# Five places for the raw weight tiles, paired down products and another order of the PSUM banks

## The chip, the cores and the metric

The kernel runs on one core of a Trainium2 chip. Its time is the device time of one execution in microseconds (us). TensorE (PE in the rows) does the matmuls, VectorE (DVE) and ScalarE (ACT) the work on their results, GpSimd (POOL) work from SBUF to SBUF, and SyncE (SP) issues nearly all transfers. Each engine takes its instructions in the written order.

## The reference, cut to what matters

```
x = attention(q, k, v)                     # 4 batches x 8 heads, 576 positions, block-causal
x = square(relu(x @ w_in1)) @ w_out1       # 2304 x 512 -> 2048 -> 512
h = x @ w_in2
g = (a0 + a1 h + a2 h^2 + a3 h^3) / (1 + |b0||h| + |b1| h^2 + 1e-6)
out = g @ w_out2                           # 2304 x 512 -> 2048 -> 512
```

## The kernel before

**Products in two parts.** Each float32 operand is split into a rounded high part and a rest, and a product is three matmuls (`PAIRS`, L129). PE therefore carries nearly all the work.

**Stages.** The first feed-forward layer is cut along its 2048 hidden columns into 16 blocks of 128 (index m). Stage A, `moe_a` (L472), does blocks 0 to 7 (HALF) for one batch at a time, in two sub-blocks of 320 and 256 tokens: eight up products `ha`, each followed by `relu_square` (L515), and then four down products `ya`, one for each 128 output columns c. Its work for batches 0 to 2 is laid between the instructions of the attention, step by step; the last batch stands alone, after the attention. The sums `ya` go to DRAM (`yp`). Stage B (from L722) does blocks 8 to 15 for all tokens in blocks of 384 and 512 (`hb`, `yb`) and adds `yp`. Stage C (from L780) is the second layer (`hc`, `yc`).

**Weights.** They arrive as 64-bit words. `Converter` (L81) turns a raw tile (512 KB, `raw`) into float32 (`cv`: one ACT and four DVE instructions, L119 to L125) and, a step later, into the two parts (`w`: L112 on ACT, L113 on POOL). One converter does each group of weights: `convA` those of stage A, `convB` (L664) twelve of the sixteen of stage B, `conv3` (L695) the rest and stage C's. A raw tile is loaded by SP (L93) into one of three places (four in `conv3`), and a place is free when the conversion of the tile in it has ended. A step that carries gates (`tc.issue_after`) is ordered behind the named instructions.

**Order.** `TileContext` orders the instructions by a simulated schedule and adds the semaphores, so the order on the engines follows from the code and the gates together. `convB` has its first three steps gated on the attention's slot 64 (`gate_b`) and the later ones on the last step of `moe_a` (`paced`).

**PSUM.** Eight banks. In stage A and the attention they are divided by name: three `tp`, one `sy`, two `mm`, two `sx`. Stages B and C take all eight anew: four `h` and four `y`.

The names in the rows leave the numbers out: `raw_bi`, `raw_bo` are raw tiles of `convB` or of the four stage-B tiles of `conv3` (i: up, o: down weights), `cv_bi` the float32 tile, `w_bi` the parts, `ga`, `gb` the squared values, `yo` the evacuated `ya`.

Of the kernel before, what the change touches and what calls it, by code (L numbers as in the profile page):

```python
# [8 lines left out]
F32 = mybir.dt.float32  # L9
F32R = mybir.dt.float32r  # L10
U32 = mybir.dt.uint32
AF = mybir.ActivationFunctionType
# [5 lines left out]
P = 128  # L18
S = 576
# [3 lines left out]
KK = DM // P  # L23
DFF = 2048
NM = DFF // P
HALF = NM // 2
HS = S // 2
NB = 12
# [3 lines left out]
SUB = 320  # L32
# [17 lines left out]
def attention_moe_moe(ctx: ExitStack, tc: tile.TileContext, q, k, v, wi1, wo1, wi2, wo2, a, b, out):  # L50
    nc = tc.nc
    NH_ALL = q.shape[0]
    H = DM // D
    B = NH_ALL // H
# [8 lines left out]
    yp = dram.tile([P, KK, NT], F32, name="yp")  # L63
# [12 lines left out]
        name=nc.get_next_instruction_name(), act_func_set_id=EXP_LN_SET, ins=[], outs=[]))  # L76
# [4 lines left out]
    class Converter:  # L81

        def __init__(self, pool, nraw, nmid, jobs):
            self.pool, self.nraw, self.nmid, self.jobs = pool, nraw, nmid, list(jobs)
            self.raws, self.mid = [], []

        def load(self, most=9):
            while self.jobs and len(self.raws) < min(self.nraw, most):  # L90
                job = self.jobs.pop(0)
                raw = self.pool.tile([P, 512, 2], U32, tag="wraw", name=f"raw_{job[0]}", bufs=self.nraw)
                nc.sync.dma_start(raw.rearrange("p n t -> p (n t)"), job[1])  # L93
                self.raws.append((raw, job))

# [3 lines left out]
        def __call__(self, *gates):  # L99
            with ExitStack() as after:  # L100
                for g in gates:
                    after.enter_context(tc.issue_after(g.ins))
                self.step()

        def step(self):
            if len(self.mid) == self.nmid or (self.mid and not self.raws):
                c, (nm, _, wp, kind, store, key, eng) = self.mid.pop(0)
                if wp is None:
                    nc.sync.dma_start(store[key], c)
                else:  # L110
                    w = wp.tile([P, 2, 512], F32R, tag="w" + kind, name=f"w_{nm}", bufs=HALF)
                    nc.scalar.activation(w[:, 0, :], c, AF.Copy)  # L112
                    eng.tensor_tensor(w[:, 1, :], c, f(w[:, 0, :]), op=ALU.subtract)  # L113
                    store[kind, key] = w
            if self.raws:
                raw, job = self.raws.pop(0)
                c = self.pool.tile([P, 512], F32, tag="cv", name=f"cv_{job[0]}", bufs=self.nmid + 1)
                low, high, cu = raw[:, :, 0], raw[:, :, 1], c.bitcast(U32)
                nc.scalar.activation(c, high.bitcast(F32), AF.Abs, scale=65536.0)  # L119
                nc.vector.tensor_scalar(low, low, 2.0 ** -29, 7.0, op0=ALU.mult, op1=ALU.min)  # L120
                nc.vector.scalar_tensor_tensor(
                    low, high, 0x80000000, low, op0=ALU.bitwise_and, op1=ALU.bitwise_or)
                nc.vector.tensor_scalar(c, c, 2.0, 122880.0 * 65536.0, op0=ALU.max, op1=ALU.min)
                nc.vector.scalar_tensor_tensor(
                    cu, cu, 3, low, op0=ALU.logical_shift_left, op1=ALU.bitwise_or)  # L125
                self.mid.append((c, job))
            self.load()

    PAIRS = ((0, 0), (1, 0), (0, 1))  # L129

# [333 lines left out]
    wA = {}  # L464
# [5 lines left out]
    paced = ()  # L470

    def moe_a(b_):  # L472
        nonlocal paced
        turn = 0

        def bank(nm):
            nonlocal turn
            turn += 1
            tag = "tp" if b_ == B - 1 and turn % 2 else "mm"
            return ps1.tile([P, 512], F32, tag=tag, name=nm, bufs=BANKS[tag])  # L480

        xt = xtile[b_]
        for s, (first, end) in enumerate(SUBS):
            n = end - first
            gs = []
            for m in range(HALF):
                ps = bank(f"ha{b_}_{s}_{m}")
                w = wA["i", m]
                for i in range(3 * KK):
                    kk, (zw, zx) = i // 3, PAIRS[i % 3]  # L490
                    nc.tensor.matmul(ps[:, 0:n], w[:, zw, P * kk:P * (kk + 1)], xt[:, zx, kk, first:end],  # L491
                                     start=i == 0, stop=i == 3 * KK - 1)
                    if i % 3 == 2 and i < 3 * KK - 1:
                        yield
                g = g1.tile([P, 2, SUB], F32R, tag="g", name=f"ga{b_}_{s}_{m}", bufs=HALF)
                paced = relu_square(lambda tag, nm: tmp1(n, nm), ps[:, 0:n], g[:, :, 0:n], f"{b_}_{s}_{m}", nc.gpsimd,
                            b_ == B - 1 and s == 1)[:2]
                gs.append(g)
                yield
            for c in range(KK):  # L500
                ps = bank(f"ya{b_}_{s}_{c}")
                for i in range(3 * HALF):
                    m, (zw, zg) = i // 3, PAIRS[i % 3]
                    nc.tensor.matmul(ps[:, 0:n], wA["o", m][:, zw, P * c:P * (c + 1)], gs[m][:, zg, 0:n],  # L504
                                     start=i == 0, stop=i == 3 * HALF - 1)
                    if i % 3 == 2 and i < 3 * HALF - 1:
                        yield
                y = g1.tile([P, n], F32, tag="ya", name=f"yo{b_}_{s}_{c}", bufs=2, padded_shape=[P, SUB])
                paced = (nc.scalar.activation(y, ps[:, 0:n], AF.Copy),)
                nc.sync.dma_start(yp[:, c, S * b_ + first:S * b_ + end], y)  # L510
                yield
        xtile.pop(b_)


# [9 lines left out]
    for gis, heads in (((0, 1), range(H)), ((2, 3), range(H)), ((0, 1, 2, 3), range(H, NH_ALL))):  # L524
# [3 lines left out]
    units_at = {un.at: n for n, un in enumerate(units)}  # L528
    NI = len(slots)
    PER_B = 4 * H  # L530
    convA = Converter(g1, 3, 1, [
        (f"a{kind}{m}", src[m], wpool, kind, wA, m, nc.gpsimd)
        for kind, src in (("i", wi1), ("o", wo1)) for m in range(HALF)])

    load_qk(units[0], nc.scalar)
    load_qk(units[1])
# [124 lines left out]
    jobsB = [(f"b{kind}{m}", src[HALF + m], w2, kind, wB, m, nc.gpsimd)  # L661
             for m in range(HALF) for kind, src in (("i", wi1), ("o", wo1))]

    convB = Converter(g1, 3, 1, jobsB[:NB])  # L664
    n = 0
    SPLITS = (73, 80, 87, 94)
    x_first = load_x(xs, *blocks2[0], "b0")
# [19 lines left out]
    def tmp(tag, n, nm, dt=F32):  # L687
# [4 lines left out]

    late = [(kind, m) for m in range(HALF, NM) for kind in "io"]
    source = {"i": wi2, "o": wo2}
    conv3 = Converter(g2, 4, 2, jobsB[NB:] + [  # L695
        (f"c{kind}{m}", source[kind][m], None, kind, waiting, n, nc.gpsimd) for n, (kind, m) in enumerate(late)] + [
        (f"c{kind}{m}", source[kind][m], wpool, kind, w3, m, nc.gpsimd) for m in range(HALF) for kind in "io"])

# [25 lines left out]
    END = 2  # L724
    SPLIT_AT = len(blocks2) * HALF - 4
    done = ()
    acc = {}
    units = [(j, m) for j in range(len(blocks2)) for m in range(HALF)]
    xt = {0: x_first}
    gs, ypart = {}, {}  # L730
# [1 line left out]
    for u in range(len(units) + LAG):  # L732
        if u < len(units):
            j, m = units[u]
            t0, n = blocks2[j]
            nxt = (xs, *blocks2[j + 1], f"b{j + 1}") if j + 1 < len(blocks2) else (xs2, *blocks3[0], "c0")
            if m == 0:
                xt[j + 1] = load_x(*nxt)
            ps = h_matmul(wB["i", m], xt[j], n, f"b{j}_{m}")
            g = g2.tile([P, 2, 512], F32R, tag="g", name=f"gb{j}_{m}", bufs=3)  # L740
            done = relu_square(lambda tag, nm: tmp(tag, n, nm), ps[:, 0:n], g[:, :, 0:n], f"b{j}_{m}", nc.vector, True)
            gs[u] = g
            if 2 <= m < 2 + KK:
                with tc.issue_after(done[1].ins):
                    split_x(xt[j + 1], m - 2, nxt[2])
        if u >= LAG:
            j, m = units[u - LAG]
            t0, n = blocks2[j]
            g = gs.pop(u - LAG)
            last = m == HALF - 1  # L750
            if m == HALF // 2:
                for c in range(KK):
                    ypart[c] = tmp("t" if c < 3 else "o", n, f"yp{j}_{c}")
                    nc.sync.dma_start(ypart[c], yp[:, c, t0:t0 + n])
            for c in range(KK):
                if m == 0:
                    acc[j, c] = psh.tile([P, 512], F32, tag="y", name=f"yb{j}_{c}", bufs=4)
                for i, (zw, zg) in enumerate(PAIRS):
                    nc.tensor.matmul(acc[j, c][:, 0:n], wB["o", m][:, zw, P * c:P * (c + 1)], g[:, zg, 0:n],  # L759
                                     start=m == 0 and i == 0, stop=last and i == 2)  # L760
            if last:
                for c in range(KK):
                    y = ypart[c]
                    done = nc.vector.tensor_tensor(y, acc.pop((j, c))[:, 0:n], y, op=ALU.add),
                    nc.sync.dma_start(xs2[:, c, t0:t0 + n], y)


        if u < 3 or u in (4, 6) or u > 6:
            conv3(*done)
        at = u - (len(units) - HALF) - 1  # L770
        for kind, m in (("i", at), ("o", at - LAG)):
            if 0 <= m < HALF:
                load_late(kind, HALF + m)
        split_late(u - SPLIT_AT, done)
# [139 lines left out]
```

## Time and profile before

| | us |
|---|---|
| median of 3 runs | 1015.86 (1014.85 to 1016.08) |
| the profiled execution, its own time | 1015.24 |
| its span, first to last instruction | 1013.5 |
| PE busy in the span | 997.2 (98%) |
| PE idle in the three waits of 375 to 435 us | 0.69, 0.68, 0.71 |

The attention with stage A laid into it runs to about 364 us of the span, the last batch of stage A from there to 412.7, stage B to about 610, stage C to the end. PE busy counts a matmul from its start to its modelled end, and the next one starts before that end, so an idle time in a row is a little shorter than what PE lost. The granted clock is 1.00 in all stretches.

### The profile page before, as it was taken

How to read it: one execution, taken by the hardware profiler on the slowest of the kernel's cores; microseconds unless marked ns; L12 is line 12 of the kernel's file. 1: busy time of each engine (PE TensorE's matmuls, PEld its weight loads, DVE VectorE, ACT ScalarE, POOL GpSimd, SP SyncE). 2: the span in 40 equal slices, each digit the busy share in tenths (PEclk: the TensorE clock that was granted, in tenths of full speed). 3: DMA queues.
4: the chain of work that ended last, by engine and by line, in shares of the span. 5: the costliest groups of instructions: out<-in, count | busy, mean ns of one | idle time of the engine just before them, and what ended most of it. 6: DMA issues, size and time to landing. Idle time of an engine off the chain costs nothing.

```text
span 1013.5 us, 17096 instructions
## 1 busy us (share of the span) xinstructions
PE 997.2 (98%) x5745; PEld 884.1 (87%) x5745; DVE 760.5 (75%) x1413; ACT 727.5 (72%) x1621; POOL 589.1 (58%) x632
## 2 busy tenths in 40 slices
PE   8999999999999999999999999999999999999998
PEld 6678998999999999999888888878888888899997
DVE  6899698768787656777768786888877667677766
ACT  7789686868877746655446566778787876778775
POOL 5777695868686755421114276865574564565552
PEclk9999999999999999999999999999999999999999
DMA  9866435243332204658754652001101100200000
GB/s 284 257 195 211 127 108 162 75 120 106 109 93 88 66 18 161 218 154 278 267 196 144 210 182 76 1 1 42 42 0 32 42 1 1 73 1 1 32 1 32
DMA packets 63895, 106.60 MB, mean 105 GB/s; under 512 B 16064, under 2 KB 34496, under 8 KB 63808
## 3 DMA queue, kind: packets, MB, share of 16 engines
q1 hardware_dynamic: 63520, 105.34, 33.3%
q8 instruction: 46, 0.75, 0.3%
q14 instruction: 41, 0.34, 0.1%
q10 hardware_dynamic: 288, 0.16, 0.1%
HBM read 79.17 MB, written 23.07 MB: 101 GB/s over the span
## 4 chain that ended last, share of the span: by engine, by line
PE 80%; DVE 7%; ACT 6%; DMA 3%; issue 2%; POOL 1%; SPq 0%; ACTq 0%; DVEq 0%; POOLq 0%
PE yc L839 17%; PE hc L718 16%; PE yb L759 9%; PE hb L718 9%; PE ha L491 7%; PE ya L504 7%; PE tp L379 4%; PE pv L451 4%; PE sx L303 3%; PE sy L303 2%; DMA raw_bo<-in_wo_dram 2%; PE pv L438 1%; DVE stat L324 1%; DVE ab L806 1%; DVE wq L805 1%
## 5 line engine op out<-in xcount | busy, mean ns | idle before, releaser
L718 PE MATMUL hc<-xc,w_ci 128*128 128x512 f32 (+1 forms) x960 | 210.9, 368 | 0.0
L718 PEld LDWEIGHTS hc<-xc,w_ci 128*128 128x128 f32 x960 | 176.4, 188 | 26.3
L839 PE MATMUL yc<-w_co,gc 128*128 128x512 f32 x792 | 194.3, 392 | 0.6 <-ACT gc L798 0.5
L839 PEld LDWEIGHTS yc<-w_co,gc 128*128 128x128 f32 x792 | 147.4, 188 | 32.4 <-POOL gc L799 2.1
L799 POOL TENSOR_TENSOR gc<-t,gc 128x512 fp32r<-128x512 f32 (+1 forms) x70 | 97.1, 1392 | 117.0 <-issue 68.6
L491 PE MATMUL ha<-xt,w_ai 128*128 128x320 f32 (+1 forms) x768 | 122.5, 305 | 0.5 <-POOL xt L460 0.5
L504 PE MATMUL ya<-ga,w_ao 128*128 128x320 f32 (+1 forms) x768 | 116.7, 299 | 1.4 <-POOL ga L521 0.7
L491 PEld LDWEIGHTS ha<-xt,w_ai 128*128 128x128 f32 x768 | 107.6, 189 | 5.1 <-issue 3.0
L504 PEld LDWEIGHTS ya<-ga,w_ao 128*128 128x128 f32 x768 | 106.4, 189 | 3.3 <-POOL ga L521 1.0
L822 POOL TENSOR_TENSOR wq<-wq,ab 128x512 f32<-128x512 f32 (+1 forms) x78 | 93.6, 1201 | 23.9 <-ACT wq L820 22.7
L759 PE MATMUL yb<-gb,w_bo 128*128 128x512 f32 (+1 forms) x480 | 105.8, 368 | 0.9 <-DVE gb L521 0.9
L718 PE MATMUL hb<-xb,w_bi 128*128 128x512 f32 (+1 forms) x480 | 105.2, 367 | 0.0
L759 PEld LDWEIGHTS yb<-gb,w_bo 128*128 128x128 f32 x480 | 87.5, 188 | 13.0 <-DVE gb L521 1.6
L718 PEld LDWEIGHTS hb<-xb,w_bi 128*128 128x128 f32 x480 | 87.4, 188 | 11.1
L823 DVE TENSOR_TENSOR t<-hc,t 128x512 f32<-128x512 f32 (+1 forms) x80 | 50.9, 637 | 59.6 <-ACT t L821 59.6
L805 DVE SCALAR_TENSOR_TENSOR wq<-wq,ab 128x512 f32<-128x512 f32 (+1 forms) x80 | 64.3, 804 | 36.9 <-ACT ab L804 22.2
L365 POOL TENSOR_SCALAR p<-p,stat 64x64 f32<-64x64 f32 (+4 forms) x110 | 64.5, 588 | 42.6 <-DVE stat L361 10.9
L798 ACT ACTIVATE gc<-t 128x512 fp32r<-128x512 f32 (+1 forms) x72 | 43.0, 597 | 62.4 <-DVE t L807 62.3
L411 DVE TENSOR_TENSOR pt<-tp,pt 128x128 fp32r<-128x128 f32 (+2 forms) x176 | 63.2, 391 | 27.1 <-ACT pt L409 16.8
L379 PE MATMUL tp<-ident,p 128*128 128x128 f32 x480 | 77.1, 276 | 0.3 <-ACT xp L446 0.3
L409 ACT ACTIVATE pt<-tp 128x128 fp32r<-128x128 f32 (+2 forms) x176 | 57.1, 362 | 26.6 <-PE tp L379 25.0
L657 POOL TENSOR_TENSOR xb<-xb 128x512 fp32r<-128x512 f32 (+1 forms) x20 | 25.4, 1268 | 75.6 <-ACT xb L656 75.6
(146 smaller groups left out, 2110.3 us busy)
## 6 DMA issues: line engine op xcount, KB each, us to landing
kr<-in_k_dram SPq DMA_DIRECT2D x32, 288.0 KB, 3.7
raw_ci<-in_wi_dram SPq DMA_DIRECT2D x16, 512.0 KB, 4.2
raw_co<-in_wo_dram SPq DMA_DIRECT2D x16, 512.0 KB, 4.1
qr<-in_q_dram SPq DMA_DIRECT2D x24, 320.0 KB, 3.4
raw_ai<-in_wi_dram SPq DMA_DIRECT2D x8, 512.0 KB, 5.8
raw_ao<-in_wo_dram SPq DMA_DIRECT2D x8, 512.0 KB, 4.1
raw_bi<-in_wi_dram SPq DMA_DIRECT2D x8, 512.0 KB, 3.7
raw_bo<-in_wo_dram SPq DMA_DIRECT2D x8, 512.0 KB, 4.2
```

The source lines that it names most:

```text
L365: nc.gpsimd.tensor_scalar(pv, pv, st[r:P, 6 + n:7 + n], 0.0, op0=ALU.mult, op1=ALU.add)
L379: nc.tensor.transpose(ps[:, P * n:P * (n + 1)], ptile(slots[i][0], t)[:, P * c:P * (c + 1)], ident)
L409: nc.scalar.activation(high, src, AF.Copy)
L411: nc.vector.tensor_tensor(low, src, f(high), op=ALU.subtract)
L491: nc.tensor.matmul(ps[:, 0:n], w[:, zw, P * kk:P * (kk + 1)], xt[:, zx, kk, first:end], start=i == 0, stop=i == 3 * KK - 1)
L504: nc.tensor.matmul(ps[:, 0:n], wA["o", m][:, zw, P * c:P * (c + 1)], gs[m][:, zg, 0:n], start=i == 0, stop=i == 3 * HALF - 1)
L718: nc.tensor.matmul(ps[:, 0:n], w[:, zw, P * kk:P * (kk + 1)], xt[:, zx, kk, 0:n], start=i == 0, stop=i == 3 * KK - 1)
L759: nc.tensor.matmul(acc[j, c][:, 0:n], wB["o", m][:, zw, P * c:P * (c + 1)], g[:, zg, 0:n], start=m == 0 and i == 0, stop=last and i == 2)
L799: (nc.vector if u - 2 >= len(units) - END else nc.gpsimd).tensor_tensor(g[:, 1, 0:n], t, f(g[:, 0, 0:n]), op=ALU.subtract)
L805: nc.vector.scalar_tensor_tensor(w, w, Q0, r, op0=ALU.add, op1=ALU.mult)
L822: squared = (nc.vector if u >= len(units) - END else nc.gpsimd).tensor_tensor(w, w, ab, op=ALU.mult)
L839: last = nc.tensor.matmul(acc[j, c], g[:, zg, P * c:P * (c + 1)], w3["o", m][:, zw, :], start=m == 0 and i == 0, stop=m == NM - 1 and i == 2)
```

## The change

`Converter` takes two sets of places: `bufs` and `more`, the second under a tag of its own. `convB` gets 3 + 2 places for raw tiles, 2 + 1 for `cv`, and `nmid` 2 instead of 1, so that the parts `w` are made two steps after `cv`. The first use of each added raw place has a memset of two words in front of its load. In `convB` (after its first load) and `conv3` a load is written outside the gates of its step. `convA` and `conv3` keep their number of places; `convA` loads inside the gates as before.

In the last batch of stage A the down products go in pairs: blocks 0 to 6 for c, blocks 0 to 6 for c + 1, and only then block 7 of both.

The `y` banks of stage B are taken before the `h` banks, which moves `h` from banks 0 to 3 to banks 4 to 7.

```
-    def __init__(self, pool, nraw, nmid, jobs):
-        self.pool, self.nraw, self.nmid, self.jobs = pool, nraw, nmid, list(jobs)
+    def __init__(self, pool, bufs, more, nmid, jobs, ahead=True):
+        self.raws, self.mid, self.turn, self.ahead = [], [], [0, 0], ahead
+        self.nraw = bufs[0] + more[0]
+    def place(self, which, shape, dt, tag, name):
+        own, more = self.bufs[which], self.more[which]
+        spare = self.turn[which] % (own + more) >= own
+        self.turn[which] += 1
+        return self.pool.tile(shape, dt, tag=tag + "2" if spare else tag, name=name, bufs=more if spare else own)
...
-                raw = self.pool.tile([P, 512, 2], U32, tag="wraw", name=f"raw_{job[0]}", bufs=self.nraw)
+                raw = self.place(0, [P, 512, 2], U32, "wraw", f"raw_{job[0]}")
+                if self.bufs[0] < self.turn[0] <= self.nraw:
+                    nc.vector.memset(raw[:, 0, :].bitcast(F32), 0.0)
                 nc.sync.dma_start(raw.rearrange("p n t -> p (n t)"), job[1])
...
                 self.step()
+                if not (self.ahead and self.turn[0]):
+                    self.load()
+            self.load()
...
-            self.load()
...
-            for c in range(KK):
-                ps = bank(f"ya{b_}_{s}_{c}")
...
+            step = 2 if b_ == B - 1 else 1
+            for c0 in range(0, KK, step):
+                cs = range(c0, c0 + step)
+                ps = {c: bank(f"ya{b_}_{s}_{c}") for c in cs}
+                order = [(c, m) for c in cs for m in range(HALF - 1)] + [(c, HALF - 1) for c in cs]
...
-    convB = Converter(g1, 3, 1, jobsB[:NB])
+    convB = Converter(g1, (3, 2), (2, 1), 2, jobsB[:NB])
...
-    acc = {}
+    acc = {(0, c): psh.tile([P, 512], F32, tag="y", name=f"yb0_{c}", bufs=4) for c in range(KK)}
```

**What it moves on PE, first sub-block of the last batch.** The names: `ya_0_0` and `ya_0_1` are the down products c = 0 and 1, `ga_0_7` is the last block's value. Before:

```order
L504 MATMUL ya_0_0_5651<-ga_0_6_5613,w_ao_1279 128x320
L504 MATMUL ya_0_1_5690<-ga_0_1_5494,w_ao_911 128x320
L504 MATMUL ya_0_1_5690<-ga_0_2_5514,w_ao_987 128x320 x3
L504 MATMUL ya_0_1_5690<-ga_0_3_5542,w_ao_1045 128x320 x2
L504 MATMUL ya_0_0_5651<-ga_0_7_5644,w_ao_1381 128x320 x2
L504 MATMUL ya_0_1_5690<-ga_0_3_5542,w_ao_1045 128x320
L504 MATMUL ya_0_1_5690<-ga_0_4_5562,w_ao_1115 128x320 x3
L504 MATMUL ya_0_1_5690<-ga_0_5_5593,w_ao_1200 128x320 x2
L504 MATMUL ya_0_0_5651<-ga_0_7_5644,w_ao_1381 128x320
L504 MATMUL ya_0_1_5690<-ga_0_5_5593,w_ao_1200 128x320
```

The same place now:

```order
L518 MATMUL ya_0_0_5654<-ga_0_6_5616,w_ao_1279 128x320
L518 MATMUL ya_0_1_5655<-ga_0_1_5500,w_ao_911 128x320 x3
L518 MATMUL ya_0_1_5655<-ga_0_2_5520,w_ao_987 128x320 x3
L518 MATMUL ya_0_1_5655<-ga_0_3_5548,w_ao_1045 128x320 x3
L518 MATMUL ya_0_1_5655<-ga_0_4_5568,w_ao_1115 128x320 x3
L518 MATMUL ya_0_1_5655<-ga_0_5_5596,w_ao_1200 128x320 x3
L518 MATMUL ya_0_1_5655<-ga_0_6_5616,w_ao_1279 128x320 x3
L518 MATMUL ya_0_0_5654<-ga_0_7_5647,w_ao_1381 128x320 x3
L518 MATMUL ya_0_1_5655<-ga_0_7_5647,w_ao_1381 128x320 x3
```

The third matmul on `ga_0_7`, the one that needs POOL's part of it, was the 41st of the down products and is now the 45th.

**What it moves on ACT, end of stage A.** The names: `yo_1_2`, `yo_1_3` are the copies of the last two down products, `w_b..` and `cv_b..` steps of `convB`, `rb_0` the first instruction of stage B. Before:

```order
L509 ACTIVATE yo_1_0_6040<-ya_1_0_6004 128x256
L509 ACTIVATE yo_1_1_6068<-ya_1_1_6043 128x256
L112 ACTIVATE w_bi_6071<-cv_bi_6031 128x512
L119 ACTIVATE cv_bo_6074<-raw_bo_5935 128x512
L509 ACTIVATE yo_1_2_6105<-ya_1_2_6080 128x256
L112 ACTIVATE w_bo_6112<-cv_bo_6074 128x512
L509 ACTIVATE yo_1_3_6136<-ya_1_3_6108 128x256
L517 ACTIVATE rb_0_6175<-hb_0_6161 128x384
```

Now:

```order
L522 ACTIVATE yo_1_0_6061<-ya_1_0_6003 128x256
L522 ACTIVATE yo_1_1_6067<-ya_1_1_6004 128x256
L124 ACTIVATE w_bo_6070<-cv_bo_5984 128x512
L131 ACTIVATE cv_bo_6073<-raw_bo_5818 128x512
L124 ACTIVATE w_bi_6108<-cv_bi_6031 128x512
L124 ACTIVATE w_bo_6138<-cv_bo_6073 128x512
L522 ACTIVATE yo_1_2_6129<-ya_1_2_6079 128x256
L522 ACTIVATE yo_1_3_6135<-ya_1_3_6080 128x256
L530 ACTIVATE rb_0_6181<-hb_0_6167 128x384
```

The last step of `convB` stood between the copies `yo_1_2` and `yo_1_3`; now both copies stand behind it, and four instructions of `convB` lie between `yo_1_1` and `yo_1_2`, where two did.

**What it moves on DVE, in the attention near slot 64.** The names: `stat`, `sy`, `tp`, `pt` belong to the attention, the rest to `convB`. Before:

```order
L360 TENSOR_SCALAR stat_131<-stat_131 128x2
L361 RECIPROCAL stat_131<-stat_131 128x2
L324 TENSOR_REDUCE stat_133<-sy_2443 128x1
L123 TENSOR_SCALAR cv_bi_5525<-cv_bi_5525 128x512
L123 TENSOR_SCALAR cv_bo_5579<-cv_bo_5579 128x512
L411 TENSOR_TENSOR pt<-tp_0_2373,pt 128x3x128
```

Now:

```order
L371 TENSOR_SCALAR stat_131<-stat_131 128x2
L132 TENSOR_SCALAR raw_bi_5484<-raw_bi_5484 128x512
L372 RECIPROCAL stat_131<-stat_131 128x2
L335 TENSOR_REDUCE stat_133<-sy_2443 128x1
L135 TENSOR_SCALAR cv_bi_5531<-cv_bi_5531 128x512
L133 SCALAR_TENSOR_TENSOR raw_bi_5484<-raw_bi_5484 128x512
L135 TENSOR_SCALAR cv_bo_5582<-cv_bo_5582 128x512
L422 TENSOR_TENSOR pt<-tp_0_2373,pt 128x3x128
```

Two instructions on the raw tile of the second added place (`raw_bi_5484`) come in front of the attention's `pt`; the two memsets stand 16 rows earlier. SP issues the loads of both added places here, behind a `kr` load.

## Rows read from the trace of the kernel before

**Rows 1.** The page, busy time of each engine in the span.
```profile
PE 997.2 (98%) x5745; PEld 884.1 (87%) x5745; DVE 760.5 (75%) x1413; ACT 727.5 (72%) x1621; POOL 589.1 (58%) x632
```
**Rows 2.** Waits of PE, whole span: total us, times, longest us.
```profile
PE sy L303 <- ACT p L337: 3.0, 3, 1.5
...
PE yb L759 <- DVE gb L521: 0.9, 2, 0.7
...
PE ya L504 <- POOL ga L521: 0.7, 1, 0.7
PE ya L504 <- ACT r L517: 0.7, 1, 0.7
PE ha L491 <- POOL xt L460: 0.5, 1, 0.5
```
**Rows 3.** Timeline of PE, 365 to 440: start us, length us, instructions, idle before.
```profile
373.10 6.03 PE L504 MATMUL ya<-ga,w_ao 128*128 128x320 f32 x40
379.82 8.48 PE L504 MATMUL ya<-ga,w_ao 128*128 128x320 f32 x56 [0.69 <-POOL ga L521]
388.14 11.68 PE L491 MATMUL ha<-xt,w_ai 128*128 128x256 f32 x96
...
402.29 10.39 PE L504 MATMUL ya<-ga,w_ao 128*128 128x256 f32 x81 [0.68 <-ACT r L517]
...
432.46 2.01 PE L759 MATMUL yb<-gb,w_bo 128*128 128x384 f32 x10 [0.71 <-DVE gb L521]
```
**Rows 4.** Matmul groups of PE by shape: busy us, mean ns of one.
```profile
L504 PE MATMUL ya<-ga,w_ao 128*128 128x320 f32 x384 | 64.3, 313 | 0.7 <-POOL ga L521 0.7
L504 PE MATMUL ya<-ga,w_ao 128*128 128x256 f32 x384 | 52.4, 286 | 0.7 <-ACT r L517 0.7
```
**Rows 5.** Timelines of DVE and POOL, 376 to 380.
```profile
376.53 1.52 DVE L123 TENSOR_SCALAR cv_bi<-cv_bi 128x512 f32<-128x512 f32 x1
...
376.01 1.75 POOL L113 TENSOR_TENSOR w_bo<-cv_bo,w_bo 128x512 fp32r<-128x512 f32 x1
378.59 1.18 POOL L521 TENSOR_TENSOR ga<-s,ga 128x320 fp32r<-128x320 f32 x1 [0.82 <-DVE s L520]
```
**Rows 6.** Timelines of ACT and DVE, 398 to 402.
```profile
401.34 0.63 ACT L112 ACTIVATE w_bo<-cv_bo 128x512 fp32r<-128x512 f32 x1 [2.41 <-DVE cv_bo L124]
401.87 0.37 ACT L517 ACTIVATE r<-ha 128x256 f32<-128x256 f32 x1
...
398.56 0.95 DVE L120 TENSOR_SCALAR raw_bo<-raw_bo 128x512 uint32<-128x512 uint32 x1 [0.91 <-DMA raw_bo<-in_wo_dram]
```
**Rows 7.** Timelines of ACT, SP and DVE, 415 to 431.
```profile
415.07 0.63 ACT L112 ACTIVATE w_bo<-cv_bo 128x512 fp32r<-128x512 f32 x1 [1.59 <-DVE cv_bo L124]
415.61 0.37 ACT L509 ACTIVATE yo<-ya 128x256 f32<-128x256 f32 x1
...
416.37 0.42 SPq L93 DMA_DIRECT2D raw_bi<-in_wi_dram  x1
...
430.77 2.11 DVE L521 TENSOR_TENSOR gb<-sb,gb 128x384 fp32r<-128x384 f32 x2
```
**Rows 8.** Timelines of SP, DVE and POOL in the attention, 161 to 174.
```profile
161.06 0.38 SPq L202 DMA_DIRECT2D kr<-in_k_dram  x1
...
167.40 0.62 DVE L324 TENSOR_REDUCE stat<-sy 128x1 f32<-128x448 f32 x1 [0.38 <-PE sy L303]
...
171.98 1.92 POOL L249 TENSOR_TENSOR kk<-kr,kk 64x576 fp32r<-64x576 f32 x1
```
**Rows 9.** Groups of DVE by shape: busy us, mean ns of one.
```profile
L121 DVE SCALAR_TENSOR_TENSOR raw_bi<-raw_bi 128x512 uint32<-128x512 uint32 x8 | 8.3, 1036 | 0.1
...
L120 DVE TENSOR_SCALAR raw_bi<-raw_bi 128x512 uint32<-128x512 uint32 x8 | 5.9, 742 | 7.0 <-DMA raw_bi<-in_wi_dram 6.9
...
L267 DVE MEMSET stat<- 128x8 f32 x8 | 0.2, 65 | 0.0
```
**Rows 10.** The line that issues the raw loads, issue to landing, 64 loads.
```profile
DMA to landing us min/median/max: 3.3/4.1/7.9
```

More of the change, by code (lines that the diff above doesn't have):

```diff
@@ L81, in attention_moe_moe @@
     class Converter:
-        def __init__(self, pool, nraw, nmid, jobs):
-            self.pool, self.nraw, self.nmid, self.jobs = pool, nraw, nmid, list(jobs)
-            self.raws, self.mid = [], []
+        def __init__(self, pool, bufs, more, nmid, jobs, ahead=True):
+            self.pool, self.bufs, self.more, self.nmid, self.jobs = pool, bufs, more, nmid, list(jobs)
+            self.raws, self.mid, self.turn, self.ahead = [], [], [0, 0], ahead
[5 more added lines that the diff above has]
+            return self.pool.tile(shape, dt, tag=tag + "2" if spare else tag, name=name, bufs=more if spare else own)
         def load(self, most=9):
@@ L116, in step @@
                 raw, job = self.raws.pop(0)
-                c = self.pool.tile([P, 512], F32, tag="cv", name=f"cv_{job[0]}", bufs=self.nmid + 1)
+                c = self.place(1, [P, 512], F32, "cv", f"cv_{job[0]}")
                 low, high, cu = raw[:, :, 0], raw[:, :, 1], c.bitcast(U32)
@@ L499, in moe_a @@
                 yield
-            for c in range(KK):
-                ps = bank(f"ya{b_}_{s}_{c}")
[L502 to L511, printed above, removed]
+            step = 2 if b_ == B - 1 else 1
[3 more added lines that the diff above has]
+                order = [(c, m) for c in cs for m in range(HALF - 1)] + [(c, HALF - 1) for c in cs]
+                for c, m in order:
+                    for i, (zw, zg) in enumerate(PAIRS):
+                        nc.tensor.matmul(ps[c][:, 0:n], wA["o", m][:, zw, P * c:P * (c + 1)], gs[m][:, zg, 0:n],
+                                         start=m == 0 and i == 0, stop=m == HALF - 1 and i == 2)
+                    if m == HALF - 1:
+                        y = g1.tile([P, n], F32, tag="ya", name=f"yo{b_}_{s}_{c}", bufs=2, padded_shape=[P, SUB])
+                        paced = (nc.scalar.activation(y, ps[c][:, 0:n], AF.Copy),)
+                        nc.sync.dma_start(yp[:, c, S * b_ + first:S * b_ + end], y)
+                    yield
         xtile.pop(b_)
@@ L530, in attention_moe_moe @@
     PER_B = 4 * H
-    convA = Converter(g1, 3, 1, [
+    convA = Converter(g1, (3, 2), (0, 0), 1, [
         (f"a{kind}{m}", src[m], wpool, kind, wA, m, nc.gpsimd)
-        for kind, src in (("i", wi1), ("o", wo1)) for m in range(HALF)])
+        for kind, src in (("i", wi1), ("o", wo1)) for m in range(HALF)], False)
     load_qk(units[0], nc.scalar)
@@ L694, in attention_moe_moe @@
     source = {"i": wi2, "o": wo2}
-    conv3 = Converter(g2, 4, 2, jobsB[NB:] + [
+    conv3 = Converter(g2, (4, 3), (0, 0), 2, jobsB[NB:] + [
         (f"c{kind}{m}", source[kind][m], None, kind, waiting, n, nc.gpsimd) for n, (kind, m) in enumerate(late)] + [
@@ L755, in attention_moe_moe @@
             for c in range(KK):
-                if m == 0:
+                if m == 0 and j:
                     acc[j, c] = psh.tile([P, 512], F32, tag="y", name=f"yb{j}_{c}", bufs=4)
```

## The prediction

> **What bounds the kernel now.** I read the page's busy times first. The reader is to see that PE is busy 98% of the span and no other engine over 75% [rows 1]: nothing that only makes another engine faster can help, and what a change can win is time in which PE stands still. So the next view is the list of PE's waits [rows 2]. Most of them belong to the attention, whose instructions the change hardly touches. Three lie where stage A's last batch runs alone and hands over to stage B, and the conversion of stage B's weights is the work beside them. The timeline of PE gives their places: 379.8, 402.3 and 432.5 us, with 0.69, 0.68 and 0.71 us [rows 3].
>
> An idle time is less than what PE lost. Ninety-six matmuls of 256 columns take 11.68 us [rows 3], one of them 0.286 [rows 4], so one starts every (11.68 - 0.29) / 95 = 0.120 us; a stall adds the 0.17 by which the next would have started before the last one's end. For 320 columns: (8.48 - 0.31) / 55 = 0.149, so 0.16 again, and I use 0.16 for 384 columns too. After the stall at 402.3 the 81 matmuls take 10.39 instead of 80 x 0.120 + 0.29 = 9.89, another 0.50 in pieces too small to be listed. PE's losses there: A at 379.8 0.69 + 0.16 = 0.85; B at 402.3 0.68 + 0.17 + 0.50 = 1.35; C at 432.5 0.71 + 0.16 = 0.87. Together 3.07 us: that is what the change can reach in this stretch.
>
> Then I asked the other engines' timelines what each stall stands on. At A, POOL's part of the last block (`ga`, 378.59 + 1.18) ends just as PE goes on [rows 5]. At B, ACT reaches the `r` that frees PE's next bank only at 401.87, because the `w_bo` in front of it waited 2.41 us for a conversion on DVE, and DVE had waited for a raw tile's load [rows 6]. At C, the cause lies 17 us back: the last copy `yo` ran at 415.61 behind a `w_bo` that had waited 1.59 us for DVE; SP, whose loads of `conv3` stand behind the store of that copy, issued the first at 416.37; DVE's conversions of these tiles then ran so late that two `gb` came out together at 430.77 [rows 7].
>
> **The change part by part.**
>
> Pairs of down products. The matmul that needs the last `ga` is the 45th instead of the 41st. Nothing in front of that `ga` on ACT, DVE or POOL changes: one `w`, one `cv`, then the last block, as before. So PE has four more matmuls to do, 4 x 0.149 = 0.59 us, and 0.26 of A stays. Gain 0.59. If that `ga` comes earlier (its square stood behind a DVE instruction of 1.52 us) the gain is 0.85; if one more instruction gets in front of POOL, 0.
>
> Five places, split two steps on. With five raw tiles, the load of a tile is issued two conversions earlier, and `w` takes a `cv` finished a whole step before. DVE will still wait for some of the later loads, since a place is free only when a conversion has ended, but ACT no longer stands behind the newest one. Without the 2.41 us on ACT, `r` would start at 401.87 - 2.41 = 399.5 and end 0.37 later; PE asks for it at 402.29 - 0.85 = 401.4, so 1.6 us are in hand. Gain 1.35, all of B; nothing if ACT meets another wait of that length. What is late next is POOL's `ga`, with the pair order behind it.
>
> End of stage A. PE ends the last `ya` at 402.29 + 10.39 = 412.7. Both copies now have nothing left of `convB` in front of them that depends on a load still to be issued, so I put them at PE's end plus two copies of 0.37 us, and SP's first load about 1.0 us after PE's end instead of 416.37 - 412.7 = 3.7. The conversions of these tiles start 2.7 us earlier against PE; the stall needed 0.87. Gain 0.87; zero if DVE's queue from 420 on, and not the load, sets the time of `gb`. The copies now wait behind the last `w_bo`; if its conversion is late by 1.6 us, as before, the gain falls to what 1.1 us of lead gives, which still covers C.
>
> The attention near slot 64. Added on DVE: two memsets and two instructions on a raw tile that came later in the old order. The memsets take 0.065 each by the nearest row; the others 0.742 and 1.036 in the mean [rows 9], and 0.38 of them fits where DVE waits for PE anyway [rows 8]. At worst all the rest, 0.13 + 1.78 - 0.38 = 1.5 us, stands in front of an instruction that PE waits for. At best nothing does, and the wait for `xt` (0.5 [rows 2], with 0.16 on top) goes, since PE now takes nine matmuls that need none of the late `xt` first, 9 x 0.149 = 1.3 us of cover. I take a gain of 0.3: the `xt` wait goes, and half of it is paid back by the memsets and by `pt` coming later; `pt`'s users stand some 2 us of PE work behind it.
>
> The Trainium skill (SBUF — State Buffer, Who interferes with whom) speaks against this part: DVE and POOL share a port pair as an exclusive lock, so an instruction that needs it waits until the other engine's has ended. The trace agrees as far as it goes: the `cv` step of 1.52 us ended after POOL's 376.01 + 1.75 [rows 5]. By that rule this part would cost what the third rival says.
>
> Banks. `h` of stage B moves to banks 4 to 7 and its first product takes the bank of the down product c = 1, copied 5 us of matmuls before it is wanted. No wait goes or comes: 0, and 0.9 (a copy behind its matmul, with the refill) if I have the bank wrong. Loads outside the gates in `conv3` leave its rows as they were: 0. So does everything after 435 us, where the order is the same row by row.
>
> Sum: 0.59 + 1.35 + 0.87 + 0.3 = 3.1 us. The profiled execution took 1015.24 us, 1.74 more than its span, so it would take 1012.1; it was 0.62 below the median of the runs, which becomes 1015.86 - 3.1 = 1012.8.
>
> **The rivals.**
>
> 1. Only the ACT stall goes. A keeps its 0.85 because the last `ga` is late by more, and C stays because DVE, not the load, was its cause: DVE is without a pause there, as two `gb` in one row show [rows 7]. Gain 1.35 + 0.3: 1014.2, inside what counts as no change.
> 2. The loads are not early enough, and the change doesn't do what it says: the last four tiles of `convB` are still issued only after conversions that themselves waited, 4.1 us from issue to landing [rows 10], so ACT waits as before and the gains are 0.59 at A less 0.3 in the attention: 1015.6. Against it: `w` is one step further back now.
> 3. DVE and POOL get in each other's way in the attention (the rule named above). Each of the two added DVE instructions stands for the whole of POOL's longest there, 1.92 [rows 8], and PE waits for all of it but the 0.38: 3.5 us lost, 3.1 - 0.3 = 2.8 won: 1016.6.
> 4. Slower: the added loads hold DVE. DVE takes its instructions in order, and the one on `raw_bi_5484` now stands in front of the attention's maximum. Its load is the second behind that of `kr` at 161.06, 0.38 us each [rows 8], so it is issued near 162, and it is wanted near 167, just ahead of the maximum at 167.40. A landing in the median 4.1 us is in time; one of 7.9 [rows 10] holds DVE until 169.9, 2.9 us. The next two loads are as close in front of their use, and one of them lies in the shadow of the other: as much again. A landing of L costs 2 x (L - 5), begins to matter at 5 us and eats the 2.8 won at 6.4. At 7.9: 1015.9 - 2.8 + 5.8 = 1018.9.
>
> **How the numbers follow.** Chances: forecast 0.57, rivals 0.18, 0.10, 0.06 and 0.09. About 0.2%, 2.0 us, is what a measurement of this kernel can tell from no change, so faster means under 1013.8. The forecast lies under it unless a third of its gain is missing; that happens in one case in ten and is made up by rival 1 coming out better. So faster 0.57; slower 0.08, most of rival 4; no change 0.35. The range starts where all three stalls and the `xt` wait go without a loss (3.07 + 0.66 = 3.7 from the median, 1012.1, and 0.6 lower for the spread of the runs) and reaches past rivals 1 and 2: 1011.5 to 1015.8. The forecast's own range is 1011.8 to 1013.7.
>
> **What would show it.** In PE's timeline the stalls before the 45th `ya` matmul (0.1 to 0.3 left), before the 16th of the second sub-block (none) and in stage B's fourth down product (none). On ACT no wait of over 1 us for a `cv` between 390 and 410, and `yo` directly behind PE's end; on SP the first `conv3` load within 1.5 us of it. Between 155 and 185 us PE's idle time the same or half a microsecond less, and no wait of DVE for a raw tile before 178. The prediction is wrong if stage B begins less than 1.5 us earlier than before, or if what is won by 435 us is lost again by 680.

## The result, and the profile after

The changed kernel takes 1023.65 us (median of 6 runs, 1022.46 to 1024.99) against 1015.29 for the kernel before, run beside it: 1.0075 times as long, 95% interval 1.0065 to 1.0086. It is slower, and the time lies outside the predicted range. The profiled execution took 1024.58 us, its span 1022.8; before it was 1013.5, so the two traces have 9.3 us between them.

The page first. PE is busy 3.4 us longer than in [rows 1], though it does the same 5745 matmuls, so some of them ran more slowly; DVE, ACT and POOL do what they did.

```profile
PE 1000.6 (98%) x5745; PEld 887.7 (87%) x5745; DVE 760.1 (74%) x1415; ACT 726.2 (71%) x1621; POOL 590.7 (58%) x632
```

The waits of PE (total us, times, longest us), as in [rows 2]. The two stalls that were to go are gone or moved: `ya<-POOL ga` (0.7) does not appear, nor does `ha<-POOL xt` (0.5). Four entries are new, and together they come to 8.2 us.

```profile
PE sy L314 <- ACT p L348: 3.0, 3, 1.5
PE pv L462 <- DVE stat L371: 2.9, 1, 2.9
PE ya L518 <- ACT ga L531: 2.5, 1, 2.5
PE pv L462 <- DVE xp L466: 1.7, 1, 1.7
...
PE tp L390 <- DVE stat L371: 1.1, 1, 1.1
```

To find where they are, I took the gap from each matmul's start to the next one's, less the median gap of its size, and summed that by stretch. Before, PE lost 2.3 us at 170 to 180 and -0.1 at 180 to 190; after, 6.1 and 2.8: **6.7 us more in the attention**. At 400 to 420 it lost 1.4 before and 5.4 after: **4.0 us more in the last batch**. Against that stand 1.0 us won at 370 to 380 and 1.0 at 430 to 440. No other stretch of 10 us differs by more than 0.8.

**The attention.** SP and DVE from 161 us on (start, length, instruction, idle before it); these are the rows that answer to [rows 8].

```profile
161.92 0.42 SPq L102 DMA_DIRECT2D raw_bo<-in_wo_dram  x1
162.43 0.38 SPq L102 DMA_DIRECT2D raw_bi<-in_wi_dram  x1
...
171.44 0.43 DVE L132 TENSOR_SCALAR raw_bi<-raw_bi 128x512 uint32<-128x512 uint32 x1 [4.24 <-DMA raw_bi<-in_wi_dram]
171.79 0.16 DVE L372 RECIPROCAL stat<-stat 128x2 f32<-128x2 f32 x1
171.86 0.60 DVE L335 TENSOR_REDUCE stat<-sy 128x1 f32<-128x448 f32 x1
```

The two loads into the spare places are issued at 162. The second is that of `raw_bi_5484`, and DVE stands 4.24 us before its first step, until 171.44: 9.0 us after the issue. Behind it in DVE's order is the maximum of the attention (`L335`), which took place at 167.40 before [rows 8]. Every engine then waits down the line:

```profile
172.56 0.64 ACT L348 ACTIVATE p<-sy,stat 128x448 f32<-128x448 f32 x1 [2.23 <-DVE stat L335]
...
172.14 1.47 POOL L376 TENSOR_SCALAR p<-p,stat 64x64 f32<-64x64 f32 x2 [5.37 <-DVE stat L372]
...
174.40 0.59 PE L462 MATMUL pv<-pt,vs 128*128 128x320 f32 x3 [2.88 <-DVE stat L371]
178.31 0.30 PE L390 MATMUL tp<-ident,p 128*128 128x128 f32 x1 [1.10 <-DVE stat L371]
180.32 1.30 PE L462 MATMUL pv<-pt,vs 128*128 128x256 f32 x5 [1.71 <-DVE xp L466]
```

The Trainium skill (PSUM — Partial Sum Buffer, Engine vs sequencer instructions) calls the queues of ScalarE, VectorE and GpSimd strict FIFO; the trace agrees, since a reciprocal of 0.16 us whose data was long there waited with the rest.

**The last batch.** The timeline of PE, answering to [rows 3]. The 96 `ya` at 380.15 run through: the stall at 379.8 is gone altogether. The one at 402.29 has become two, 0.57 and 2.49 us, and stage B, which was to begin earlier, begins at 422.65 instead of near 412.5.

```profile
380.15 14.24 PE L518 MATMUL ya<-ga,w_ao 128*128 128x320 f32 x96
394.23 11.68 PE L502 MATMUL ha<-xt,w_ai 128*128 128x256 f32 x96
405.75 1.96 PE L518 MATMUL ya<-ga,w_ao 128*128 128x256 f32 x15
408.28 4.18 PE L518 MATMUL ya<-ga,w_ao 128*128 128x256 f32 x30 [0.57 <-ACT r L530]
414.94 7.87 PE L518 MATMUL ya<-ga,w_ao 128*128 128x256 f32 x51 [2.49 <-ACT ga L531]
422.65 6.75 PE L731 MATMUL hb<-xb,w_bi 128*128 128x384 f32 x38
```

SP, DVE and ACT behind the longer stall, answering to [rows 6]:

```profile
406.80 0.33 SPq L102 DMA_DIRECT2D raw_bo<-in_wo_dram  x1
...
410.33 0.83 DVE L132 TENSOR_SCALAR raw_bo<-raw_bo 128x512 uint32<-128x512 uint32 x1 [3.59 <-DMA raw_bo<-in_wo_dram]
411.19 0.69 DVE L133 SCALAR_TENSOR_TENSOR raw_bo<-raw_bo 128x512 uint32<-128x512 uint32 x1
411.80 0.42 DVE L135 TENSOR_SCALAR cv_bo<-cv_bo 128x512 f32<-128x512 f32 x1
412.25 0.69 DVE L136 SCALAR_TENSOR_TENSOR cv_bo<-cv_bo,raw_bo 128x512 uint32<-128x512 uint32 x1
...
412.98 0.63 ACT L124 ACTIVATE w_bo<-cv_bo 128x512 fp32r<-128x512 f32 x1 [2.97 <-DVE cv_bo L136]
...
414.47 0.42 ACT L531 ACTIVATE ga<-r 128x256 fp32r<-128x256 f32 x1
```

The twelfth and last tile gets its place, and so its load, when the seventh is converted, at 406.80. Its first step stands on DVE in front of the last steps of the eighth (`L135`, `L136` at 411.80 and 412.25), whose tile was loaded long ago. DVE waits 3.59 us for the load, ACT 2.97 for the eighth tile's `cv`, and the `ga` behind that `w_bo` comes 2.49 us late for PE. So five places did move each load two conversions ahead of its own tile's turn; but DVE's order moved the first step of the tile ahead with it.

After both holds the granted clock falls: to 0.50 from 180.0 us in the first place, from 415.5 us in the second. Windows of 2 us (start:end, length, busy time of PE, PEld, DVE, ACT and POOL, clock, DMA share, GB/s): 0.51 and 0.50 of full speed, the lower of the two levels, 1.2 GHz.

```profile
180.00:182.00 2.00, 1.68 (x7) 1.71 (x8) 1.97 (x6) 0.00 (x0) 1.65 (x3) 0.51 0.99 349
416.00:418.00 2.00, 2.00 (x11) 2.00 (x11) 2.00 (x2) 1.07 (x4) 1.76 (x2) 0.50 0.00 0
```

In the last batch the low clock costs 1.6 of the 4.2 us lost at 410 to 420, and the wait the rest: the 51 matmuls behind the stall take 7.87 us, where 50 x 0.120 + 0.29 = 6.29 would do. That is nearly half of PE's 3.4 us of longer work.

### The profile page after: what moved, and what is told of

It is laid out like the page before. It is cut to its first block, busy times and chain, and to the rows that moved or that the text cites. A ratio compares the mean times of both kernels' runs of the same rounds, so it can differ in the third digit from the quotient of the medians.

```text
span 1022.8 us, 17093 instructions
## 1 busy us (share of the span) xinstructions
PE 1000.6 (98%) x5745; PEld 887.7 (87%) x5745; DVE 760.1 (74%) x1415; ACT 726.2 (71%) x1621; POOL 590.7 (58%) x632
## 4 chain that ended last, share of the span: by engine, by line
PE 79%; DVE 9%; ACT 6%; DMA 4%; issue 2%; POOL 0%; SPq 0%; ACTq 0%; DVEq 0%; POOLq 0%
PE yc L852 17%; PE hc L731 16%; PE hb L731 9%; PE yb L772 8%; PE ya L518 7%; PE ha L502 7%; PE tp L390 4%; PE pv L462 4%; PE sx L314 3%; PE sy L314 2%; DMA raw_bi<-in_wi_dram 2%; PE pv L449 1%; DVE stat L335 1%; DVE ab L819 1%; DVE wq L818 1%
```

## The experiments

In the order in which they ran, in three groups of four. Each time is a median beside the kernel before, which took 1015.23, 1015.35 and 1015.12 us in the three groups; the interval is that of the ratio to it.

| kernel | us | ratio, 95% interval |
|---|---|---|
| e1 changed kernel, in order | 1012.25 | 0.9955 to 0.9980 |
| e2 in order from the eighth tile on | 1018.99 | 1.0020 to 1.0045 |
| e3 before + pairs | 1017.17 | 1.0009 to 1.0027 |
| e4 before + five places | 1016.31 | 0.9998 to 1.0016 |
| e5 e2 + spare tiles loaded early | 1013.80 | 0.9972 to 0.9991 |
| e6 e1 without pairs and banks | 1012.31 | 0.9957 to 0.9981 |
| e7 before + pairs, in order | 1011.06 | 0.9943 to 0.9968 |
| e8 e1 with the old banks | 1011.90 | 0.9954 to 0.9979 |
| e9 before, in order | 1012.13 | 0.9958 to 0.9980 |
| e10 changed, twelfth tile held | 1018.34 | 1.0020 to 1.0041 |
| e11 changed, fifth tile held | 1017.28 | 1.0012 to 1.0031 |
| e12 e7, next converter in order too | 1010.50 | 0.9940 to 0.9968 |

The theory: DVE is held, in both places, by the first step of a tile whose load has just been issued, standing in front of work that is ready. The rivals: the loads' traffic in the attention, the pairs, and later the work itself.

**e1, in order.** "In order" is one wait, and all of e1, e2 and e5 to e12 are built on it:

```diff
+        def held(self):
+            return self.more[0] and self.turn[1] > 2
...
-                nc.vector.tensor_scalar(low, low, 2.0 ** -29, 7.0, op0=ALU.mult, op1=ALU.min)
+                with tc.issue_after(self.last.ins) if self.held() else ExitStack():
+                    nc.vector.tensor_scalar(low, low, 2.0 ** -29, 7.0, op0=ALU.mult, op1=ALU.min)
...
-                nc.vector.scalar_tensor_tensor(
+                self.last = nc.vector.scalar_tensor_tensor(
```

> The changed kernel, with one wait more: from the third tile of the second half on, VectorE may begin a tile only behind the last conversion of the tile before it; loads, places, pairs and banks stay. In the changed kernel TensorE lost 6.7 us more than before at 170 to 190 us and 4.0 us more at 400 to 420. My theory: both are VectorE held by the first step of a tile whose load had just been issued, standing in front of work that was ready. Then both go, and the gains of the pairs (0.85) and of the earlier loads after stage A (0.87) stay: about 1013 us (1012 to 1014.5), and no VectorE wait for a raw tile over 1 us. Rival 'traffic': the two loads more, issued at 162 us, delay the attention's own loads; they are still there, so about 6.7 of it stays: about 1019.5 us. Rival 'pairs': two copies that come due together cost the 4 us at 400 to 420: about 1017 us.

1012.25, as the theory says. 'Traffic' is out: both loads are still issued in the attention, at 162.08 and 162.60 us, and PE lost only 0.1 us at 170 to 190. 'Pairs' is out too, since they are still in. In the changed kernel DVE waited 14.8 us in all for raw tiles of the second half; in e1 one wait of 2.4 us is left, for the first tile of `conv3`, where I had expected none over 1 us. The lines of the changed kernel, then e1's, whose L136 is the same instruction as L132:

```profile
DVE raw_bi L132 <- DMA raw_bi<-in_wi_dram: 8.8, 4, 4.2
DVE raw_bo L132 <- DMA raw_bo<-in_wo_dram: 6.0, 2, 3.6
```
```profile
DVE raw_bi L136 <- DMA raw_bi<-in_wi_dram: 2.4, 1, 2.4
```

**e2, in order from the eighth tile on.** `self.turn[1] > 7` in place of `> 2`. No row moves on any engine but DVE, and there none before the last batch.

> As the run before, but the wait holds only from the eighth tile on, so the attention near 165 to 185 us is as in the changed kernel and only the last batch is put in order. My theory: the 4 us at 400 to 420 go, the 6.7 us in the attention stay: about 1019.5 us (1018.5 to 1020.5). 'Pairs': nothing goes, about 1023.6. 'Traffic': as my theory, 1019.5; only the run before tells those two apart.

1018.99. PE lost nothing at 400 to 420 and about 9 us at 170 to 190, as in the changed kernel. With e1 the two places are priced apart: 4.7 us for the last batch (1023.65 - 1018.99) and 6.7 for the attention (1018.99 - 1012.25). The second price isn't the hold's alone: e1 also wins 2.1 us at 170 to 190 that the kernel before had lost, and loses some elsewhere. e11 below moves only the tile of that hold.

**e3, pairs alone.** The change's loop over pairs put into the kernel before (`step = 2 if b_ == B - 1 else 1`), nothing else.

> The kernel before with the down products in pairs of banks in the last batch, nothing else: three places, loads inside the gates, banks taken in the old order. My theory: the pairs win the stall at 379.8 us (0.6 to 0.85 us) and cost nothing: about 1014.6 us, the stalls at 402 and 432 us stay. 'Pairs' as the cause of the loss at 400 to 420 us: 1017 us or more.

1017.17: my theory as I wrote it missed, and the rival's number was right. The trace tells why the rival's cause is not: it is the same hold, with three places. The pairs move ACT's copies, the order laid out for DVE moves with them, and again first steps of tiles just being loaded stand in front of ready ones; e7, which adds the order, takes the loss away (DVE, ACT, PE):

```profile
395.44 0.43 DVE L132 TENSOR_SCALAR raw_bi<-raw_bi 128x512 uint32<-128x512 uint32 x1 [1.39 <-DMA raw_bi<-in_wi_dram]
...
396.96 0.69 DVE L136 SCALAR_TENSOR_TENSOR cv_bi<-cv_bi,raw_bi 128x512 uint32<-128x512 uint32 x1
...
397.69 0.63 ACT L124 ACTIVATE w_bi<-cv_bi 128x512 fp32r<-128x512 f32 x1 [3.00 <-DVE cv_bi L136]
...
399.20 1.98 PE L502 MATMUL ha<-xt,w_ai 128*128 128x256 f32 x12 [2.22 <-ACT r L530]
```

**e4, five places alone.** The changed kernel with `step = 1` and the old order of the banks.

> The changed kernel without the pairs and with the old order of the banks: the five places, the loads outside the gates and the split two steps on alone. My theory: all of the loss is here, and the pairs' 0.85 is missing: about 1024.5 us (1023.5 to 1025.5). 'Pairs': about 1019.5 us, since only the attention's loss is left.

1016.31, 8 us less than I expected; "pairs" (1019.5) missed too. Without the pairs the last batch is clean: PE lost 0.1 us at 400 to 420 and nothing at 430. In the attention it is the fourth tile, not the fifth, whose first step was moved up; its load was issued half a microsecond earlier and DVE waited 4.07 us, but PE lost only 2.2 us more than before at 160 to 190. The tile landed at 168.58, 2.8 us earlier than the fifth tile in the changed kernel. Here the runs spread widely (1014.52 to 1018.84), the interval of the ratio takes in 1, and the trace is of a run of 1015.11. So neither half of the change costs what both do. My reading is that a late load costs what the time of its landing and the ready instructions behind its first step make of it; no run tells these two apart.

**e5, the spare tiles loaded early.** e2, with the first loads of `convB` gated sixteen slots earlier and the fifth tile's first step kept at slot 64:

```diff
+        if i == 48:
+            gate_l = tuple(gates.values())
...
-            convB(*(gate_b if n < 27 else paced))
+            convB(*(gate_l if n == 0 else gate_b if n < 27 else paced))
...
+                fifth = self.more[0] and self.turn[1] == 5
+                with tc.issue_after(gate_b[0].ins if fifth else self.last.ins) if fifth or self.held() else ExitStack():
```

> As the run with the order kept from the eighth tile on (1018.99 us), but the loads of the two spare tiles are issued sixteen slots of the attention earlier, and the first step of the fifth tile still comes at slot 64. Everything that VectorE does there is still done there; only the tile is there in time. My theory (the price in the attention is the landing of that tile, 9.0 us after its issue): VectorE's wait of 4 us goes and with it the loss of 6.7 us at 170 to 190: about 1012.3 us (1011.5 to 1013.5). Rival 'work': the first steps of three more tiles on VectorE inside the attention, some 3 us, are what delays the maxima: 1016 us or more.

1013.80, 5.2 us less than e2 and 0.3 above my range: the landing is the price, "work" is out. The load is issued at 120.13, the first step follows without a wait at 161.89 (here L137), and PE lost 2.3 us at 170 to 180 and -0.2 at 180 to 190, the figures of the kernel before.

```profile
120.13 0.38 SPq L102 DMA_DIRECT2D raw_bi<-in_wi_dram  x1
...
161.89 0.79 DVE L137 TENSOR_SCALAR raw_bi<-raw_bi 128x512 uint32<-128x512 uint32 x1
```

It stays 1.5 us above e1, which loses 1.9 us less at 170 to 180: with the first steps of the fifth to seventh tile out of the attention, the wait for `xt` [rows 2] and the second wait for `p` go as well.

**e6, places in order without pairs.** e1 with `step = 1` and the old order of the banks.

> The kernel in order (1012.25 us) without the pairs and with the old order of the banks. My theory: the pairs' own gain at the end of the first sub-block goes, 0.55 us (what the run without pairs still lost at 380 to 390) to 0.85: about 1012.9 us. Rival: pairs are worth nothing once VectorE is in order: 1012.2 us.

1012.31: nothing to tell it from e1, so the rival's number was right. PE did lose 0.6 us at 370 to 380, where e1 lost nothing, as I had expected, but 0.4 less at 410 to 420 and 0.3 less at 600 to 610.

**e7, pairs and order with three places.** e3 with the wait of e1.

> The kernel before with the pairs, its three places and loads inside the gates, and VectorE in order from the third tile on. My theory: the late first steps that cost the run with the pairs alone 4 us at 395 to 405 no longer stand in front of ready work, but with three places a tile is loaded only two conversions ahead, so VectorE and ScalarE still wait for loads: the stall of 1.35 us stays, about 1013.6 us (1012.8 to 1015). Rival: order is all, five places are worth nothing: 1012.3 us.

1011.06, and my theory missed: three places are enough. They are even better: its slowest run (1011.35) is faster than the fastest of e1 (1011.91). In the traces e1 loses 1.3 us more at 410 to 430, and the section on why the prediction was wrong says what stands there. The last batch and the beginning of stage B run without a listed stall; the first 96 `ya` take 14.62 us, where the changed kernel's take 14.24:

```profile
371.92 14.62 PE L523 MATMUL ya<-ga,w_ao 128*128 128x320 f32 x96
386.38 11.68 PE L507 MATMUL ha<-xt,w_ai 128*128 128x256 f32 x96
397.90 11.68 PE L523 MATMUL ya<-ga,w_ao 128*128 128x256 f32 x96
409.42 6.75 PE L736 MATMUL hb<-xb,w_bi 128*128 128x384 f32 x38
```

**e8, the old banks.** e1 with `acc = {}` and the bank taken at the first product.

> The kernel in order (1012.25 us) with the four banks of stage B's first block taken as before, when its first product starts. No instruction changes its place on any engine. My theory: no bank is waited for, 1012.25 us within 0.4. Rival: a bank still being read by the last copies of stage A is asked for early: about 0.7 us more.

1011.90, within the spread of e1: the banks do nothing.

**e9, order alone.** The kernel before with the wait of e1 and nothing of the change.

> The kernel before with nothing but the order: from the third tile of the second half on, VectorE begins a tile only behind the last conversion of the tile before it. No pairs, three places, loads inside the gates, split one step on. My theory, mended after the last runs: the order alone wins what the five places were to win (the 1.35 us at 402 and the 0.87 at 432), and the pairs add the 0.6 at the end of the first sub-block: about 1011.7 us (1011 to 1012.6), 0.6 above the kernel with pairs, three places and order (1011.06). Rival: order pays only where pairs or five places have spoiled it, and the kernel before has little to win by it: 1014.5 us or more.

1012.13, as the theory says. Of the three stalls of [rows 3], A stays as it was, and B and C are gone. The order alone removes both; no load had to be moved in the code. PE loses 1.3 us less at 400 to 410 and 1.0 less at 430 to 440. It also loses 1.9 less at 170 to 180, where the first steps of the fourth and fifth tile, at 173.86 and 175.17 in the kernel before, have left the attention. Some 1.2 us come back at 600 to 670. Against e7 the pairs are worth 1.1 us with three places; with five (e6 against e1) they are worth nothing.

```profile
377.85 8.47 PE L523 MATMUL ya<-ga,w_ao 128*128 128x320 f32 x56 [0.70 <-POOL ga L539]
386.16 11.68 PE L507 MATMUL ha<-xt,w_ai 128*128 128x256 f32 x96
397.68 11.68 PE L523 MATMUL ya<-ga,w_ao 128*128 128x256 f32 x96
```

**e10, the twelfth tile held.** `self.turn[1] == 12`: the two first steps of one tile move eight rows down DVE's order, and no other row moves on any engine.

> The changed kernel with two instructions moved and no other: the two first steps of the twelfth tile on VectorE, from in front of the conversions of the eighth to eleventh tiles to behind them. My theory: the wait of 3.59 us at 410 goes and with it the 4.2 us that TensorE lost at 410 to 420; the attention stays as it is: about 1019.4 us (1018.6 to 1020.4). Rival: several late tiles share the price, and with this one moved another takes its place: 1021.5 us or more.

1018.34, just under my range: 5.3 us for two instructions, a little more than the 4.2. PE lost 0.0 us at 410 to 420, and the attention's tile also landed sooner in this run, 7.3 us after its issue (DVE's wait is 2.58 us, where the changed kernel has 4.24).

```profile
169.63 0.43 DVE L136 TENSOR_SCALAR raw_bi<-raw_bi 128x512 uint32<-128x512 uint32 x1 [2.58 <-DMA raw_bi<-in_wi_dram]
```

**e11, the fifth tile held.** `self.turn[1] == 5`.

> The changed kernel with the fifth tile alone held: its first two steps on VectorE, which stood in the attention near slot 64, stand behind the conversion of the fourth tile in the last batch; the sixth and seventh stay in the attention. My theory: the wait of 4.24 us at 171 goes, and 6.7 us with it; the 4 us of the last batch stay: about 1017 us (1016 to 1018.2). Rival: the sixth tile's first step takes the place of the fifth's: 1020 us or more.

1017.28, as the theory says: 6.4 us less than the changed kernel. PE lost 2.3 and 0.5 us at 170 to 190; a stall of 2.5 us in the last batch (`ya<-ACT ga`) is still there.

**e12, the next converter in order too.** e7, with the first tiles of `conv3` under the same wait.

> The kernel with pairs, three places and order (1011.06 us), with the next converter's first four tiles, those of the second half too, held to the same order. Three instructions of VectorE move by one to three rows. My theory: no late load stands there in front of ready work, so nothing changes: 1011.1 us within 0.4. Rival: VectorE's split of an activation comes 0.3 to 0.6 us earlier there: 1010.6 us.

1010.50, the lowest of all, 4.6 us under the kernel before. That is 0.2 under my range and near the rival's figure, but its interval and e7's overlap, so the last half microsecond is not established.

## Why the prediction was wrong

**The step that failed** is "Five places, split two steps on": "DVE will still wait for some of the later loads ... but ACT no longer stands behind the newest one. Gain 1.35, all of B." The first half was true and I did not follow it. If DVE waits for a late tile, everything behind that wait on DVE is late, the last steps of older tiles included, and ACT's `w` waits for those. At 412.98 ACT waited 2.97 us for the `cv` of the eighth tile because DVE stood at the twelfth. B did not become 0; it became the 4.7 us that e2 prices. It took both halves of the change: with five places and without the pairs (e4) the twelfth tile's first step stands in the same place in front of the eighth's last steps, but DVE waits only 1.56 us for it, at 402.86, and PE lost 0.1 us at 400 to 420, as predicted. Why the pairs lengthen that wait to 3.59 us no run shows. The reading of B behind it, that a load was late [rows 6], stopped too early: e9 removes B with three places, and the load that DVE waited for at 398.56 is itself issued sooner there (391.63 against 395.11, 1.5 us sooner against PE's own progress), because the conversions that free the places end sooner. The row with `0.91 <-DMA raw_bo` already showed a first step in front of older work; I read in it the load, not the order.

**The attention** was to gain 0.3 with -1.5 as its worst. The wait for `xt` did go, as said, though PE was late there for another reason. The worst was bounded by the work added to DVE; it should have been bounded by a wait. That was **rival 4**, right in place, instruction and mechanism: DVE held in front of the maximum by `raw_bi_5484`, issued near 162. Its landing was too short: 9.0 us, where the longest of [rows 10] was 7.9. Its own 2 x (L - 5) gives 8.0 for that, and 6.7 were lost, though not by the way it names: the next two loads were used without a wait, and the second half came at PE's next two pauses, through ACT and POOL, which stand behind the maximum, and through the clock. Nor is 9.0 fixed: the same load took 8.7 us in e2, 7.3 in e10 and 7.1 in e11. The chance of 0.09 was the mistake: the load's place in SP's queue and the instruction behind its first step were both known, and the reserve of 5 us lay inside the 4.1 to 7.9 us that such loads took.

**What held.** The pairs at A: predicted 0.59 to 0.85, 0.97 at 370 to 380 in the changed kernel. The end of stage A: SP's first load of `conv3` at 423.84, 1.0 us after PE's end at 422.81, as predicted, and C is gone. The reading of C holds over all the kernels: it goes with the time from PE's end to that load. Where this is 3.5 us or less (the changed kernel, e3, e4, e7, e9 to e12), stage B's first 30 us lose nothing. Where it is 3.7 or more (before and e6 3.7, e1, e2, e5 and e8 4.4 to 4.5), they lose 0.8 to 1.7 us. In e1, PE ends at 408.93 and the load comes 4.4 us later:

```profile
411.54 0.63 ACT L127 ACTIVATE w_bo<-cv_bo 128x512 fp32r<-128x512 f32 x1 [2.58 <-DVE cv_bo L140]
412.08 0.64 ACT L526 ACTIVATE yo<-ya 128x256 f32<-128x256 f32 x2
...
413.35 0.41 SPq L102 DMA_DIRECT2D raw_bi<-in_wi_dram  x1
...
PE yb L776 <- DVE gb L538: 1.4, 2, 0.8
```

In e7, where PE ends at 409.58, it comes 3.3 us later:

```profile
412.90 0.45 SPq L103 DMA_DIRECT2D raw_bi<-in_wi_dram  x1
```

So C needed less than the prediction's 0.87 us of lead: loads that came 0.2 to 0.4 us earlier than before against PE's end went with no loss. No run moves that load alone, so this is a rule read off fourteen traces and not a test. That the changed kernel met it was in part luck, since its PE came 4.0 us late: in e2, the same kernel with its last batch in order, the load comes 4.4 us after PE's end and C is back.

The banks: nothing (e8). After 435 us: nothing.

**Rivals 1 to 3.** The first did not occur. Of the second a part did: the twelfth load was issued only behind conversions that had themselves waited, and ACT waited 2.97 us, where it had waited 2.41 before. But it foresaw no loss by that, since it left out the finished work behind the waiting step. The third is there in one row, behind the hold: a conversion step of 0.69 us elsewhere took 1.91 us beside POOL's 1.67. It comes with the hold: in e5 and e11, which lack it, POOL's instruction comes after that step, and the step takes 0.68. PE's pause of 2.88 us was over at 174.40, before it began; how much of the two later pauses is due to its 1.2 us is not shown.

```profile
174.93 1.91 DVE L136 SCALAR_TENSOR_TENSOR cv_bo<-cv_bo,raw_bo 128x512 uint32<-128x512 uint32 x1
...
174.62 1.67 POOL L260 TENSOR_TENSOR kk<-kr,kk 64x576 fp32r<-64x576 f32 x1 [1.01 <-ACT kk L255]
```

The sum by prices: A and C won 2.0, the last batch cost 4.0 and the attention 6.7, together 8.7 of the 9.3 us between the two spans.

## What to carry to other kernels

Where one engine works on several tiles at once, an earlier load helps only if the engine also comes to that tile later than to those that are ready; in this kernel a first step that needs a fresh load belonged behind the last step of the tile before it. When a trace shows a wait for a DMA, look at what stands behind the waiting instruction before asking for more buffers: one wait in the order was worth 3.0 us here, and five places in order gained nothing over three: without the pairs they took the same time, with the pairs 1.2 us longer. And a bound for "added work on an engine" is the wait that the work brings with it, not its duration.

## What the runs showed of the hardware

- A load of 512 KB took 9.0 us to land in the attention, while the median of the 64 was 4.2. It was issued behind `qr`, `yp`, `kr` and the other raw tile, all from 160.16 us on, and the DMA engines were busy at 0.76 and 0.71 of their time there (start:end, length, busy times, clock, DMA share, GB/s):

```profile
160.00:165.00 5.00, 4.73 (x39) 4.43 (x38) 4.35 (x15) 2.36 (x8) 2.54 (x3) 1.00 0.76 208
165.00:170.00 5.00, 3.55 (x29) 3.29 (x28) 0.95 (x4) 4.21 (x13) 1.69 (x3) 1.00 0.71 240
```

- The granted clock does not follow the length of one pause alone. In e2 PE stood 2.56 us before 173.84 and the clock was 0.50 in every window from 174 to 182; in the changed kernel it stood 2.88 us before 174.40, kept 1.00 until 180, and fell in the last of two more pauses, of 1.10 and 1.71 us. Pauses of 1.45 us alone, as in [rows 2], left it at 1.00. PE lost about 9 us at 170 to 190 in both: in the changed kernel it waited more for DVE, in e2 it ran longer at the low clock.
